# Sixteen weight pieces at sixteen offsets: moving the operands of a matmul kernel by bytes

## The chip, the cores and the metric

The kernel runs on one core of one Trainium2 chip. The metric is the device time of one execution in microseconds (us), as the median of the runs shown. Engines: PE is TensorE (PEld its weight loads), DVE VectorE, ACT ScalarE, POOL GpSimd, SP SyncE.

## What is computed

A retention layer (attention without softmax, with a decay by distance), followed by two feed-forward layers of 512 to 2048 to 512 over 2304 tokens:

```python
scores = scale * np.matmul(q, k.transpose(0, 1, 3, 2))   # 4 x 8 heads, 576 x 576, head_dim 64
ret = scores * Dmat                                      # gamma ** (row - column), causal
x = np.matmul(ret, v)                                    # laid out as (2304, 512)
h = x @ w_in;  x = np.maximum(0.01 * h, h) @ w_out       # first layer
h = x @ w_in2; x = (h - np.tanh(h)) @ w_out2             # second layer
```

The four weight matrices arrive as 64-bit floats and are narrowed on the chip.

## The kernel before

Every product of the two layers is made of three matmuls in float32r (fp32r): each operand is split into a high part and a low part, and high x high, low x high and high x low are summed in PSUM. x lies in SBUF for the whole kernel as `xh` and `xl`, [128, 4, 2304] each, and `acc` holds the sum over groups.

**Weights.** Each matrix is cut into 16 pieces f of 128 x 512 elements: `w_in` by its output columns, `w_out` by its rows. A piece is loaded (`load_piece`, on the SP queue), narrowed by five instructions (`narrow_ops`, lines 111 to 156, on DVE and partly ACT), and split by `split_piece` (line 171): ACT writes the high part to `wp[:, 0, :]` (line 174), POOL the low part to `wp[:, 1, :]` (line 175). `wp` is a tile of the pool `wring` with four buffers for the input pieces (tag w0) and four for the output pieces (tag w1). So four input and four output pieces, one "group", are in place at a time; a layer has four groups. Some narrowed pieces of the second layer are written to DRAM during the first and fetched back later.

**Layers.** A step (m, g, t0, n, f) is layer m, group g, a block of n tokens (512, or 256 for the last block) and one piece f of the group. `h_mm` (line 187, matmul in line 194) makes 12 matmuls, 4 slices of x by 3 products, with the weight slice as the stationary operand and `xh` or `xl` as the moving one. `act_a` and `chain` make from it `g`, high and low. `o_mm` (line 245, matmul in line 266) makes 12 matmuls with the output piece: in the first layer the weight slice is stationary and g moves, in the second g is stationary and the whole 512-wide row of the piece moves (6 matmuls where n is 256). `evac` adds into `acc`. In the loop of `layers`, step s issues `h_mm(s)` and then `o_mm(s - 2)`, so PE alternates between 12 input and 12 output matmuls, in an order that is written out by hand (`tc.manual_schedule`). Group 0 of the first layer has the 512-block and the 256-block alone in this loop; every other group has four 512-blocks and the 256-block.

**Retention and early units.** The 16 head pairs are worked off in `retention`. Beside the later ones, the first six 256-token blocks of group 0 of the first layer are done in 12 "units" of two pieces each: `unit_h` (24 matmuls of 256 columns, line 516; pieces 0 and 1 in even units, 2 and 3 in odd ones) and `unit_o` (24, line 541), with g tiles of a pool of their own.

**Places in SBUF.** Tiles lie one after another in the order of their pools, rounded to 32 bytes. In each partition the program has: the Pool DMA scratch at byte 0 (16,384 bytes), four constants and `qb` (32 bytes each), `xh` at 16,544, `xl` at 53,408, `acc` at 90,272, the eight `wp` buffers at 127,136 + 4096 s for s = 0 to 7 (s = 0 to 3 for input pieces, 4 to 7 for output pieces), the stage, and then the pools of either phase: the layers' `g` at 188,576 and two more 4096 apart, the early units' `g` at 213,088 and 217,184. The input pieces f mod 4 = 0, 1, 2, 3 get the buffers s = 0, 3, 2, 1, the output pieces 4, 7, 6, 5. All DMAs are issued with `nc.sync` or `nc.scalar`; none by POOL.

Of the kernel before, what the change touches and what calls it, by code (L numbers as in the profile page):

```python
# [11 lines left out]
F32R = mybir.dt.float32r  # L12
# [6 lines left out]
P = 128  # L19
CH = 128  # L20

TANH_T = 0.5
RHO_C = 0.0020447001866573740
RHO_V = 5.4327571340882842
# [7 lines left out]
def retention_moe_moe(  # L34
# [16 lines left out]
    nc = tc.nc  # L51
# [12 lines left out]
    wring = ctx.enter_context(tc.tile_pool(name="wring", bufs=GF))  # L64
# [105 lines left out]

    def split_piece(key):
        wf = half.pop(key)
        wp = wring.tile([P, 2, 512], F32R, tag=f"w{key[1]}", name="wp")
        nc.scalar.activation(out=wp[:, 0, :], in_=wf, func=AF.Copy)  # L174
        nc.gpsimd.tensor_tensor(  # L175
            out=wp[:, 1, :], in0=wf, in1=wp[:, 0, :].bitcast(F32), op=ALU.subtract
        )
        wt[key] = wp
# [132 lines left out]
    def piece_ops(keys, split=True, spare=()):  # L311


        ops, late = [], []
        for j, key in enumerate(keys):
            part = narrow_ops(key)
            if j + 2 < len(keys):
                part.append(lambda k=keys[j + 2]: load_piece(k))
            ops += part[:3] + late + part[3:]
            late = [lambda k=key: split_piece(k)] if split else []  # L320
            if key in spare:
                late = [lambda k=key: keep_piece(k)]
        return ops + late


    def retention():
        with ExitStack() as ac:
# [265 lines left out]
            nc.vector.memset(qb[:, 0:1], -RHO_V * math.sqrt(RHO_C))  # L593
            nc.vector.memset(qb[:, 1:2], -TANH_T * TANH_T)
            nc.scalar.activation(out=qb[:, 3:4], in_=qb[:, 2:3], func=AF.Tanh)
# [31 lines left out]
    def layers():  # L627
        with ExitStack() as mc:
# [35 lines left out]
            for s in range(n_early, end):  # L664
                h_mm(s)
                tight = s >= end - GF
                if tight:
                    act_a(s)
                if s > n_early:
                    chain(s - 1)  # L670
                if not tight:
                    act_a(s)
                if n_early <= s - LAG < end - GF:
                    o_mm(s - LAG)
                ops = plan.get(s, [])
                for op in ops[:4]:
                    op()
                if n_early <= s - LAG < end - GF:
                    evac(s - LAG)
                for op in ops[4:]:  # L680
                    op()
                for key in splits.get(s, ()):
                    split_piece(key)
# [79 lines left out]
```

## Time and profile before

| what | value |
|---|---|
| runs | 892.84 and 893.32 us, median 893.08 |
| profiled execution, first to last instruction (span) | 889.4 us |
| what lies around the span (median less span) | 3.7 us |
| busy in the span: PE, PEld | 863.9, 740.8 us |
| busy in the span: DVE, ACT, POOL | 532.8, 374.3, 422.5 us |
| mean granted TensorE clock | 0.995 |

The span is that of one execution under the profiler; the times above it are of runs without it. The end of a matmul's record is modelled, so that records overlap: the pace of matmuls is read from the distance of their starts. In the chain of waits, a piece "x12" is twelve instructions one behind another, and its time is their share of the chain.

### The profile page before, as it was taken

The numbers are of one execution on the slowest core, as the hardware profiler recorded it, in microseconds if no ns is written. First come the engines' busy times: TensorE is split into PE (matmuls) and PEld (weight loads), VectorE is DVE, ScalarE is ACT, GpSimd is POOL, SyncE is SP. The second block draws the span as 40 slices with busy tenths as digits, with TensorE's granted clock in tenths as the row PEclk, the third lists the DMA queues.
The fourth block names the chain that finished last, engine by engine and source line by source line (L and its number), as shares of the span: only waits on it lengthen the run. The fifth ranks groups of instructions, "written<-read, shape, count | busy, mean of one in ns | idle before, by whom it ended". The sixth has DMA issues, their size and how long they took to land.

```text
span 889.4 us, 13456 instructions
## 1 busy us (share of the span) xinstructions
PE 863.9 (97%) x5152; PEld 740.8 (83%) x5152; DVE 532.8 (60%) x880; ACT 374.3 (42%) x751; POOL 422.5 (48%) x340
## 2 busy tenths in 40 slices
PE   6669999999999999999999999999999999999998
PEld 5669999988888889888888888888888888888886
DVE  6964343698888788865652555444545655555454
ACT  2333222242122212233324665675466555565553
POOL 4644432264233622363224644585457744585443
PEclk9989999999999999999999999999999999999999
DMA  8743342233464335531121200020001000001111
GB/s 299 237 141 118 108 132 78 71 108 106 131 185 149 120 128 148 173 107 48 48 83 39 57 1 1 8 76 13 1 1 47 13 1 1 1 1 48 48 48 71
DMA packets 28576, 70.97 MB, mean 80 GB/s; under 512 B 3297, under 2 KB 3681, under 8 KB 28513
## 3 DMA queue, kind: packets, MB, share of 16 engines
q1 hardware_dynamic: 27936, 69.74, 24.5%
q8 instruction: 40, 0.66, 0.3%
q10 hardware_dynamic: 576, 0.38, 0.1%
q14 instruction: 24, 0.19, 0.1%
HBM read 59.10 MB, written 11.01 MB: 79 GB/s over the span
## 4 chain that ended last, share of the span: by engine, by line
PE 92%; DVE 3%; ACT 1%; DMA 1%; POOL 1%; issue 1%; SPq 0%; ACTq 0%; POOLq 0%
PE h L194 41%; PE a L266 40%; PE a L541 4%; PE x_b L516 3%; PE o L463 1%; PE sc L402 1%; PE o L475 1%; DVE cw L148 1%; DVE pt L417 1%; DMA kv<-in_vn 1%; POOL wp L175 1%; PE x_c L435 1%; DMA qk<-in_qT 1%; PE x_a L408 0%; DVE st L445 0%
## 5 line engine op out<-in xcount | busy, mean ns | idle before, releaser
L194 PE MATMUL h<-xh,wp 128*128 128x512 f32 (+1 forms) x1184 | 355.2, 366 | 0.0
L194 PEld LDWEIGHTS h<-xh,wp 128*128 128x128 f32 x1184 | 216.1, 189 | 37.0
L194 PE MATMUL h<-xl,wp 128*128 128x512 f32 (+1 forms) x592 | 216.9, 366 | 0.0
L266 PE MATMUL a<-wp,g 128*128 128x512 f32 x864 | 209.4, 390 | 0.2 <-POOL g L240 0.2
L266 PEld LDWEIGHTS a<-wp,g 128*128 128x128 f32 x864 | 161.1, 188 | 33.8 <-POOL g L240 1.0
L266 PE MATMUL a<-g,wp 128*128 128x512 f32 (+1 forms) x816 | 175.6, 364 | 0.0
L240 POOL TENSOR_TENSOR g<-v,g 128x512 fp32r<-128x512 f32 (+1 forms) x80 | 94.8, 1186 | 144.6 <-ACT g L239 144.5
L266 PEld LDWEIGHTS a<-g,wp 128*128 128x128 f32 x816 | 141.4, 189 | 24.6
L240 POOL TENSOR_TENSOR g<-a,g 128x512 fp32r<-128x512 f32 (+1 forms) x68 | 88.0, 1294 | 154.9 <-ACT g L208 141.5
L207 ACT ACTIVATE a<-h 128x512 f32<-128x512 f32 (+1 forms) x68 | 37.3, 548 | 227.0 <-PE h L194 226.1
L175 POOL TENSOR_TENSOR wp<-cw,wp 128x512 fp32r<-128x512 f32 x64 | 90.9, 1430 | 76.1 <-ACT wp L174 75.7
L194 PEld LDWEIGHTS h<-xl,wp 128*128 128x128 f32 x592 | 111.6, 189 | 18.5
L148 DVE SCALAR_TENSOR_TENSOR cw<-st,cw 128x512 uint32<-128x512 uint32 x128 | 115.2, 900 | 3.8
L233 DVE TENSOR_TENSOR h<-h,t 128x512 f32<-128x512 f32 (+1 forms) x80 | 51.5, 644 | 107.3 <-ACT t L217 107.3
L292 DVE TENSOR_TENSOR acc<-a,acc 128x512 f32<-128x512 f32 (+1 forms) x114 | 73.8, 662 | 66.8 <-PE a L266 66.7
L239 ACT ACTIVATE g<-v 128x512 fp32r<-128x512 f32 (+1 forms) x80 | 47.1, 589 | 145.4 <-DVE v L237 144.3
L218 POOL TENSOR_TENSOR v<-t,u 128x512 f32<-128x512 f32 (+1 forms) x80 | 94.8, 1185 | 14.2 <-ACT t L217 13.8
L234 DVE SCALAR_TENSOR_TENSOR v<-q,v 128x512 f32<-128x512 f32 (+1 forms) x80 | 55.5, 694 | 55.2 <-POOL v L218 54.1
L237 DVE COPY_PREDICATED v<-mk,h 128x512 f32<-128x512 uint32 (+1 forms) x80 | 54.9, 686 | 8.2
L219 ACT ACTIVATE q<-u,qb 128x512 f32<-128x512 f32 (+1 forms) x80 | 54.5, 681 | 0.0
L222 ACT ACTIVATE mk<-u,qb 128x512 f32<-128x512 f32 (+1 forms) x80 | 54.2, 677 | 0.0
L216 ACT ACTIVATE u<-h 128x512 f32<-128x512 f32 (+1 forms) x80 | 43.6, 545 | 19.4 <-PE h L194 18.9
(60 smaller groups left out, 774.5 us busy)
## 6 DMA issues: line engine op xcount, KB each, us to landing
st<-in_w1i SPq DMA_DIRECT2D x16, 512.0 KB, 3.6
st<-in_w1o SPq DMA_DIRECT2D x16, 512.0 KB, 3.5
st<-in_w2i SPq DMA_DIRECT2D x16, 512.0 KB, 4.0
st<-in_w2o SPq DMA_DIRECT2D x16, 512.0 KB, 4.0
kept<-cw SPq DMA_DIRECT2D x24, 256.0 KB, 4.3
cw<-kept SPq DMA_DIRECT2D x24, 256.0 KB, 2.7
kv<-in_vn SPq DMA_DIRECT2D x16, 320.0 KB, 5.1
qk<-in_qT SPq DMA_DIRECT2D x16, 288.0 KB, 4.0
```

The source lines that it names most:

```text
L148: nc.vector.scalar_tensor_tensor(out=t["w"], in0=t[src], scalar=scalar, in1=t["w"], op0=op, op1=ALU.bitwise_or)
L175: nc.gpsimd.tensor_tensor(out=wp[:, 1, :], in0=wf, in1=wp[:, 0, :].bitcast(F32), op=ALU.subtract)
L194: nc.tensor.matmul(out=ps[:, :n], lhsT=w[:, wi, cs], rhs=x[:, kk, t0:t0 + n], start=kk == 0 and i == 0, stop=kk == KK - 1 and i == 2,)
L218: nc.gpsimd.tensor_tensor(out=v[:, :n], in0=t_[:, :n], in1=u[:, :n], op=ALU.mult)
L219: nc.scalar.activation(out=q[:, :n], in_=u[:, :n], func=AF.Square, scale=math.sqrt(RHO_C), bias=qb[:, 0:1])
L222: nc.scalar.activation(out=mk[:, :n], in_=u[:, :n], func=AF.Relu, bias=qb[:, 1:2])
L233: nc.vector.tensor_tensor(out=h, in0=h, in1=t_, op=ALU.subtract)
L234: nc.vector.scalar_tensor_tensor(out=v, in0=q, scalar=RHO_A, in1=v, op0=ALU.add, op1=ALU.mult)
L237: nc.vector.copy_predicated(out=v, mask=mk.bitcast(U32), data=h)
L240: nc.gpsimd.tensor_tensor(out=gt[:, 1, :n], in0=v, in1=gt[:, 0, :n].bitcast(F32), op=ALU.subtract)
L266: nc.tensor.matmul(out=o, lhsT=l, rhs=r, start=f == 0 and i == 0 and d % pack == 0, stop=f == GF - 1 and i == 2 and (d + 1) % pack == 0, s ...
L292: nc.vector.tensor_tensor(out=dst, in0=a, in1=dst, op=ALU.add)
```

## The change

Each piece gets a buffer of 1136 elements a partition (4544 bytes) in place of 1024, and begins in it at an offset of its own, by f: 0, 16, 32, ... 112 bytes for f = 0 to 7, then 128, 256, 384, 4, 8, 192, 320, 448. ACT, POOL and PE address the same [128, 2, 512] view as before, at that offset. To make room, the scratch for DMAs of POOL, at the bottom of SBUF, shrinks from 16,384 to 1024 bytes.

```diff
+PLACES = (0, 4, 8, 12, 16, 20, 24, 28, 32, 64, 96, 1, 2, 48, 80, 112)
...
     def split_piece(key):
         wf = half.pop(key)
-        wp = wring.tile([P, 2, 512], F32R, tag=f"w{key[1]}", name="wp")
+        at = PLACES[key[2] % len(PLACES)]
+        room = wring.tile([P, 1024 + max(PLACES)], F32R, tag=f"w{key[1]}", name="wp")
+        wp = room[:, at:at + 1024].rearrange("p (i d) -> p i d", i=2)
         nc.scalar.activation(out=wp[:, 0, :], in_=wf, func=AF.Copy)
...
-    nc = bacc.Bacc("TRN2", target_bir_lowering=False, num_devices=1)
+    nc = bacc.Bacc("TRN2", target_bir_lowering=False, num_devices=1, dynamic_dma_scratch_size=1024)
```

## Rows read from the trace of the kernel before

**Rows 1.** The page: its span, the busy time, and the chain by line.

```profile
span 889.4 us, 13456 instructions
...
PE 863.9 (97%) x5152; PEld 740.8 (83%) x5152; DVE 532.8 (60%) x880; ACT 374.3 (42%) x751; POOL 422.5 (48%) x340
...
PE h L194 41%; PE a L266 40%; PE a L541 4%; PE x_b L516 3%; PE o L463 1%; PE sc L402 1%; PE o L475 1%; DVE cw L148 1%; DVE pt L417 1%; DMA kv<-in_vn 1%; POOL wp L175 1%; PE x_c L435 1%; DMA qk<-in_qT 1%; PE x_a L408 0%; DVE st L445 0%
```

**Rows 2.** Chain in order of time (start, us, what): both layers.

```profile
203.56 2.72 PE a L266 x12
206.28 2.72 PE h L194 x12
...
614.45 2.72 PE a L266 x12
```

**Rows 3.** Chain in order of time: an early unit.

```profile
94.80 2.88 PE x_b L516 x24
97.67 2.74 PE a L541 x24
```

**Rows 4.** Timeline of PE, 98 to 99.95 us (start, us, engine, line, count).

```profile
97.75 2.43 PE L541 MATMUL a<-g,wp 128*128 128x256 f32 x20
```

**Rows 5.** The instructions of tile wp: min/median/max in ns.

```profile
L541 PEld LDWEIGHTS a<-g,wp x288: 186/188/338, 50.3 to 161.7; 128*128 128x128 f32 x144
L541 PE MATMUL a<-g,wp x288: 276/276/582, 50.4 to 161.8; 128*128 128x256 f32 x144
L516 PEld LDWEIGHTS x_b<-xh,wp x192: 186/192/193, 36.7 to 153.8; 128*128 128x128 f32 x192
L516 PE MATMUL x_b<-xh,wp x192: 277/283/388, 36.8 to 154.0; 128*128 128x256 f32 x192
...
L174 ACT ACTIVATE wp<-cw x64: 615/630/645, 21.9 to 798.6; 128x512 fp32r<-128x512 f32 x64
L175 POOL TENSOR_TENSOR wp<-cw,wp x64: 1264/1300/1783, 23.0 to 799.3; 128x512 fp32r<-128x512 f32 x64
```

**Rows 6.** Timeline, line view and windows, line 541 near 59 us (0.50 is PEclk).

```profile
58.78 1.70 PE L541 MATMUL a<-g,wp 128*128 128x256 f32 x7
...
L541 PE MATMUL a<-g,wp x8: 415/415/420, 58.6 to 60.1; 128*128 128x256 f32 x8
...
59.00:60.10 1.10, 1.10 (x7) 0.50 0.00 0
```

**Rows 7.** Timeline, 97.3 to 97.6 us: a matmul and the next one's weight load.

```profile
97.27 0.28 PE L516 MATMUL x_b<-xl,wp 128*128 128x256 f32 x1
97.27 0.19 PEld L516 LDWEIGHTS x_b<-xh,wp 128*128 128x128 f32 x1
```

**Rows 8.** The page's groups of matmuls of the layers.

```profile
L194 PE MATMUL h<-xh,wp 128*128 128x512 f32 (+1 forms) x1184 | 355.2, 366 | 0.0
...
L194 PE MATMUL h<-xl,wp 128*128 128x512 f32 (+1 forms) x592 | 216.9, 366 | 0.0
L266 PE MATMUL a<-wp,g 128*128 128x512 f32 x864 | 209.4, 390 | 0.2 <-POOL g L240 0.2
...
L266 PE MATMUL a<-g,wp 128*128 128x512 f32 (+1 forms) x816 | 175.6, 364 | 0.0
```

**Rows 9.** Chain in order of time: 512-wide steps behind 256-wide ones.

```profile
173.44 1.43 PE a L266 x12
174.88 2.75 PE h L194 x12
```

**Rows 10.** Chain in order of time: the end of the last early unit.

```profile
160.88 1.18 PE a L541 x10
```

**Rows 11.** What PE waited for: us in total, times, longest.

```profile
PE a L541 <- ACT wp L174: 4.9, 1, 4.9
```

**Rows 12.** Timeline of PE, 174.7 to 177.4 us; five matmuls from first to last.

```profile
174.71 0.40 PE L194 MATMUL h<-xh,wp 128*128 128x512 f32 x1
...
175.87 0.61 PE L194 MATMUL h<-xh,wp 128*128 128x512 f32 x2
```

## The prediction

> **What bounds the kernel now.** I read the page first: of a span of 889.4 us TensorE (PE) is busy 863.9, and the chain of work that ended last lies on PE for the two big lines 194 and 266 (41% and 40%), with lines 541 and 516 next [rows 1]. The other engines are busy 60% or less, so only PE's own pace can move the end by per cents. Second, the chain in order of time. In both layers a step of 12 matmuls, 512 columns wide, takes 2.72 us, the same for line 194 and line 266, for first layer and second [rows 2]: 226.7 ns a matmul. The granted clock is 1.0 there (the 2.4 GHz level), so 512 columns at one a cycle are 213.3 ns; 13.3 ns a matmul are something else, and that is what an address could change.
>
> Third, the same operation at 256 columns, where the kernel happens to hold two relations of addresses. Line 516 (input matmuls of the early units) takes 2.88 us for 24, or 120.0 ns each; line 541 (output matmuls of the same units) takes 2.74 us for 24 [rows 3], and within such a run 20 matmuls span 2.43 us [rows 4], the last of them being 0.276 long by itself [rows 5], so (2.43 - 0.276) / 19 = 113.4 ns each. Bare streaming would be 256 / 2.4 = 106.7. The excess is 13.3 on line 516 and 6.7 on line 541, with the same width, type, number of products and weight buffers. The tile view has it too: the median matmul record is 283 ns on 516 and 276 on 541, the weight load 192 against 188 [rows 5].
>
> What differs is where the operands lie. In the program's own allocation xh and xl begin at byte 160 modulo 512 of a partition, the eight weight buffers also at 160 (they are 4096 apart), the layers' g also at 160, but the early units' g at 96. Call "distance" the start of the weight operand minus the start of the x or g operand, modulo 512. All slices step by multiples of 512, and the pace doesn't depend on which slice it is; so distance 0 costs 13.3 ns and distance 64 costs 6.7. At the lower clock level (granted 0.50, 1.2 GHz) line 541 took (1.70 - 0.415) / 6 = 214 ns a matmul [rows 6], which is bare streaming (256 / 1.2 = 213.3): two streams at a fixed relation that do not meet. I read the excess as the weight load of the next matmul, which starts as the running one does (both at 97.27 us) [rows 7], meeting the moving stream in the memory, once at distance 64 and twice at distance 0. That reading is inferred from two distances only.
>
> **The change, part by part.** No instruction, wait, DMA or queue order is added or moved. Three things change.
>
> The smaller scratch moves every tile down by 15,360 bytes, 30 x 512. No DMA in the kernel is issued by POOL. The larger buffers (8 x 448 bytes more) push what lies behind them by 11,776 bytes in all, 23 x 512. So x and both g stay at 160, 160 and 96: cost nothing.
>
> The weight pieces move. Buffers are now 4544 bytes apart, which is 64 short of a multiple of 512, so buffer s adds -64 s to the offset in PLACES. The buffers are taken in the order 0, 3, 2, 1 by the input pieces f mod 4 = 0, 1, 2, 3, and 4, 7, 6, 5 by the output pieces. That gives, for f = 0 to 15, input distances 0, 336, 416, 496, 64, 400, 480, 48, 128, 64, 256, 452, 8, 0, 192, 384, and output distances (sign aside) 256, 80, 160, 240, 320, 144, 224, 304, 384, 320, 0, 196, 264, 256, 448, 128. I take 64 bytes or more either way as far enough to save 6.7 ns, and less as saving nothing.
>
> Input: f = 0 to 3 have 7 steps each in the layers (2 + 5, as six blocks went to the early units), the others 10; 148 steps x 12 = 1776 matmuls, which are the 1184 + 592 of the page [rows 8]. Far enough are f = 1, 2 (14 steps) and 4, 5, 8, 9, 10, 14, 15 (70): 84 x 12 = 1008 matmuls. Output: 864 + 816 = 1680 [rows 8], all but f = 10, which has 5 x 12 + 4 x 12 + 6 = 114: 1566 matmuls. Together 2574 x 6.67 ns = 17.2 us. The early units add f = 1 and 2 of line 516, 2 x 6 x 12 = 144 matmuls, 1.0 us; line 541 would go from distance 64 to 320, 144, 224, 304, no change. All of it lies on the chain [rows 1, 3].
>
> Against that stands a start cost. When the relation changes between two runs of matmuls, the pace takes some matmuls to settle: line 541's 24 take 2.74 us and not 24 x 113.4 = 2.72, so 20 ns [rows 3, 4]; a 512-wide step behind a 256-wide one takes 2.75 and not 2.72 [rows 2, 9], so 30. Now input and output steps alternate at constant distance; then nearly each of 296 steps begins at a new one: 296 x 0.020 = 5.9 us, bounds 0 and 296 x 0.030 = 8.9.
>
> The saving is bounded too. The last run of line 541, which began after PE had stood idle, kept 1.18 / 10 = 118 ns at the same distance 64 [rows 10], a saving of only 2 ns; by that the sum would be 2718 x 2 = 5.4 us. I take 6.67, because every other run at the full clock shows 113, and because the layers, like these, have PE never idle. No row shows a 512-wide matmul at another distance: the bounds for it are 0 and the whole 13.3.
>
> The fine offsets: f = 11 and 12 begin 4 and 8 bytes off. No row shows such an operand. A weight load of 188 ns [rows 5] has 226.7 to hide in; as moving operand of the second layer (2 x 54 matmuls) the nearest dear row is the lower clock's pace, 100 ns more per 256 columns, so 0 to 21 us; I take 0, as the rows for aligned slices are nearer. The writers of the pieces, ACT 630 ns and POOL 1300 [rows 5], are hidden under the matmuls, except in the first group, where PE waited up to 4.9 us at once for them [rows 11]; if they became slower by a tenth, that is 0.5 us. I take 0.
>
> Sum: -17.2 - 1.0 + 5.9 = -12.3. The profiled span is 889.4 and the runs' median 893.08, so 3.7 lie around the span and stay. Span 877.1, time 880.8, say 881. With the bounds of the start cost and of the saving the case's own range is 875 to 891.
>
> **The rivals.** *Nothing changes at 512 columns.* The 13.3 ns would then be a fixed cost of a matmul with a new weight, and 541's 113 a matter of 256-wide matmuls, where load and stream are equally long. For it: 2.72 in every full step whatever the buffer. Against it: all those steps have distance 0, and 512 and 256 show the same 13.3. Time 893, less 1.0 at most. The Trainium skill sides with this rival: "TensorE: Matmul & The Clock Gate", in the section "Step-by-step: what each phase is for", gives TensorE two independent read ports, so that loading the next weights takes nothing from the running matmul; by that the sum is 0. The 283 against 276 ns of the trace speak against it, as far as two addresses can.
>
> *More is saved.* Near pieces gain also, and nothing is lost at the starts: (1776 + 1680 + 288) x 6.67 = 25 us, 868; with the start costs gone alone, 875; if the far ones lost all 13.3, 857. For it: the clean 214 at the lower clock. Against it: distance 64 still costs 6.7. The same page (section "Back-to-back issue gap") has N / 2.4 + 2.5 ns, 215.8 at 512; by that floor 3456 x 10.9 = 37.7 us would go, an estimate that no run here shows.
>
> *Slower.* Some distances are worse than 0. The mechanism is seen where a 512-wide step follows a 256-wide one: five matmuls from 174.71 to 175.87 us, 232 ns each [rows 12], 5.3 more than settled. If the streams meet oftener at mid distances, such matmuls keep 232. All 3456 so: +18.3, time 911; a third gaining and two thirds losing, with the start cost: -7.7 + 12.2 + 5.9, time 904. It decides from where under 44% of the matmuls gain (5.3 / 12), or 58% with the start cost. Against it: the one other distance seen is better.
>
> **How the numbers follow.** Forecast case 0.38, nothing changes 0.20, more is saved 0.27, slower 0.15. The range 867 to 900 leaves out the far end of the third case and the upper half of the last. Faster by over 2% (under 875.2; about what a measurement here can tell from no change) is nearly all of the third case and a little of the first: 0.29; slower by over 2% (over 911) the worst of the last case or dear fine offsets: 0.07; within 2% the rest, 0.64.
>
> **What would show it.** In the changed chain, steps of line 194 and 266 should no longer all take 2.72 us: far pieces 2.64 plus up to 0.03, near ones 2.72, sorted by f and the same in both layers. Line 516's 24 should fall for the f = 1 and 2 halves; line 541 should stay at 2.74. Steps of 2.72 everywhere make the distance no cause; steps over 2.75 would show worse distances, and over 3 us for f = 11 or 12 on line 266 of the second layer dear fine offsets. A wait of PE for wp in the layers would mean that ACT or POOL slowed down.

## The result: slower by 1.5%, and the profile after

The changed kernel takes 906.28 us (906.24 and 906.32) where the kernel before took 893.08; the ratio is 1.0149 with a 95% interval of 1.0120 to 1.0179. The forecast was 881, in a range of 867 to 900: wrong in sign, and outside the range.

The page of the changed kernel, to be read against [rows 1]:

```profile
span 904.5 us, 13456 instructions
...
PE 877.8 (97%) x5152; PEld 741.9 (82%) x5152; DVE 529.0 (58%) x880; ACT 376.2 (42%) x751; POOL 418.6 (46%) x340
...
PE h L197 41%; PE a L269 40%; PE a L544 4%; PE x_b L519 3%; PE sc L405 1%; PE o L478 1%; PE o L466 1%; DVE cw L149 1%; DVE pt L420 1%; DVE cw L138 1%; POOL wp L178 1%; PE x_c L438 1%; DVE st L448 0%; DMA qt_sb<-in_qtab 0%; ACT bd L394 0%
```

The span grew by 15.1 us and PE's busy time by 13.9, with the same instructions and the same shares of the chain (lines 194, 266, 516, 541 are now 197, 269, 519, 544). Nothing new is waited for: PE itself became slower. The chain in order of time, inside the first layer, answers to [rows 2]:

```profile
273.61 2.80 PE a L269 x12
276.41 2.79 PE h L197 x12
279.20 2.80 PE a L269 x12
282.00 2.80 PE h L197 x12
```

Steps of 2.72 us have become 2.80: 233 ns a matmul in place of 226.7, though the pieces here (f = 4 to 7) lie at input distances of 64, 112, 32 and 48 either way and output distances of 192, 144, 224 and 208. By windows (PE busy first), the layers are the stretch from 164.2 us on, and from 161.9 on in the kernel before:

```profile
164.20:900.10 735.90, 735.73 (x3457) 609.27 (x3456) 442.54 (x667) 328.12 (x626) 350.51 (x284) 1.00 0.20 62
```

```profile
161.90:885.00 723.10, 722.92 (x3457) 609.29 (x3456) 448.13 (x667) 326.11 (x626) 354.51 (x284) 1.00 0.20 63
```

The layers grew by 12.8 us of the 15.1, at the same granted clock of 1.00. The start of the layers lies 2.3 us later, but over the runs of this study it lies anywhere between 161.6 and 164.2 us, whatever the distances. From the distance of matmul starts in the layers, the 2880 matmuls of 512 columns took 654.3 us before and 667.8 after (+13.5), the 576 of 256 columns 68.9 and 68.1 (-0.8). By piece, most 512-wide steps take 2.75 to 2.80 us. For seven pieces the matmuls come back to the old 226.7 ns before a step ends, some at its start and some only after ten slower ones: at distance 0 (input pieces 0 and 13, output piece 10), at 256 (input piece 10, output pieces 0 and 13) and at 16 the other way, which is 496 (input piece 3). One step stands against any rule by distance alone: input piece 5 (distance 400), whose steps take 2.79 or 2.80 us, ran once in the second layer at 226.7 ns from its first matmul to its last. The chain has it first, and then the next block's step with the same piece:

```profile
599.31 2.72 PE h L197 x12
...
621.59 2.80 PE h L197 x12
```

The early units, in the chain, answer to [rows 3]:

```profile
96.66 2.83 PE x_b L519 x24
99.49 2.84 PE a L544 x24
```

Here the 256-wide input matmuls became a little faster (2.88 to 2.83), and the output ones, which the forecast left at 2.74, slower.

### The profile page after: what moved, and what is told of

It is laid out like the page before. It is cut to its first block, busy times and chain, and to the rows that moved or that the text cites. A ratio compares the mean times of both kernels' runs of the same rounds, so it can differ in the third digit from the quotient of the medians.

```text
span 904.5 us, 13456 instructions
## 1 busy us (share of the span) xinstructions
PE 877.8 (97%) x5152; PEld 741.9 (82%) x5152; DVE 529.0 (58%) x880; ACT 376.2 (42%) x751; POOL 418.6 (46%) x340
## 4 chain that ended last, share of the span: by engine, by line
PE 92%; DVE 4%; ACT 1%; POOL 1%; issue 1%; DMA 0%; ACTq 0%; POOLq 0%
PE h L197 41%; PE a L269 40%; PE a L544 4%; PE x_b L519 3%; PE sc L405 1%; PE o L478 1%; PE o L466 1%; DVE cw L149 1%; DVE pt L420 1%; DVE cw L138 1%; POOL wp L178 1%; PE x_c L438 1%; DVE st L448 0%; DMA qt_sb<-in_qtab 0%; ACT bd L394 0%
## 5 line engine op out<-in xcount | busy, mean ns | idle before, releaser
L197 PE MATMUL h<-xh,wp 128*128 128x512 f32 (+1 forms) x1184 | 359.1, 369 | 0.0
L269 PE MATMUL a<-wp,g 128*128 128x512 f32 x864 | 213.4, 394 | 0.2 <-POOL g L243 0.2
L269 PE MATMUL a<-g,wp 128*128 128x512 f32 (+1 forms) x816 | 178.3, 367 | 0.0
L178 POOL TENSOR_TENSOR wp<-cw,wp 128x512 fp32r<-128x512 f32 x64 | 87.7, 1378 | 87.2 <-ACT wp L177 87.0
L237 DVE SCALAR_TENSOR_TENSOR v<-q,v 128x512 f32<-128x512 f32 (+1 forms) x80 | 51.3, 641 | 51.4 <-POOL v L221 50.4
```

The source lines that it names most:

```text
L178: nc.gpsimd.tensor_tensor(out=wp[:, 1, :], in0=wf, in1=wp[:, 0, :].bitcast(F32), op=ALU.subtract)
L197: nc.tensor.matmul(out=ps[:, :n], lhsT=w[:, wi, cs], rhs=x[:, kk, t0:t0 + n], start=kk == 0 and i == 0, stop=kk == KK - 1 and i == 2,)
L237: nc.vector.scalar_tensor_tensor(out=v, in0=q, scalar=RHO_A, in1=v, op0=ALU.add, op1=ALU.mult)
L269: nc.tensor.matmul(out=o, lhsT=l, rhs=r, start=f == 0 and i == 0 and d % pack == 0, stop=f == GF - 1 and i == 2 and (d + 1) % pack == 0, s ...
```

## The experiments

### All pieces at one distance: 0, or 64

Against the changed kernel (the second has `at = 16`, elements of 4 bytes):

```diff
-        at = PLACES[key[2] % len(PLACES)]
-        room = wring.tile([P, 1024 + max(PLACES)], F32R, tag=f"w{key[1]}", name="wp")
+        at = 0
+        room = wring.tile([P, 1152], F32R, tag=f"w{key[1]}", name="wp")
```

> The changed kernel with every piece at the start of its buffer, buffers 4608 bytes apart (9 x 512), the scratch still small: every distance between a weight operand and its x or g operand is 0 modulo 512, as before. Distance theory (the pace depends on the distance, and 0 is a good one for 512 columns): 12-matmul steps of 2.72 us and 893 us in all, within 2 us. Rival (larger buffers, smaller scratch or the shifted addresses cost the time): 906 us, as the changed kernel.

> As the run before, but every piece 64 bytes into its buffer: one and the same distance (64) everywhere. Distance theory: 512-wide matmuls at 231 to 234 ns in all steps, 256-wide ones at 113 to 118; 2880 x 6 ns = +17 us, less 576 x 5 ns = 3 us in the layers and 1 us in the early units: 904 to 909 us. Start-cost rival (only the change of distance from step to step costs): no step differs from its neighbour, so 893 or less. The piece's own place (rival: only where the piece lies counts) expects the same as the distance theory; the fourth run tells these apart.

Measured: at 0, 892.45 us, ratio 0.9995 (0.9986 to 1.0005); at 64, 906.16 us, ratio 1.0139 (1.0124 to 1.0154). The chain at 0, and then at 64:

```profile
201.20 2.72 PE h L197 x12
203.92 2.72 PE a L269 x12
```

```profile
201.34 2.80 PE h L197 x12
204.14 2.80 PE a L269 x12
```

Larger buffers, the small scratch and the shifted addresses cost nothing; a constant distance of 64 costs all that the sixteen different ones did. So the loss is not the price of going from one distance to another. And 64 is where the forecast expected a gain: at 256 columns it is one (the early units' input matmuls, at 64):

```profile
95.39 2.74 PE x_b L519 x24
98.13 2.85 PE a L544 x24
```

2.88 fell to 2.74 on line 519, and line 544, now at distance 128, rose from 2.74 to 2.85. At 512 columns the same distance of 64 is bad. Nor does 64 always give 113 ns at 256 columns: in this run the 256-wide matmuls of the first layer took 113.5 ns, those of the second layer (line 197) 117.8.

### One distance for each group: a table

From here on the diffs are against the kernel with all pieces at 0, where nothing else is said.

```diff
-        at = 0
+        at = (0, 4, 8, 16, 24, 32, 48, 60)[key[0] * 4 + key[2] // GF]
```

The second kernel has (0, 1, 2, 64, 40, 44, 52, 56).

> One offset for all eight pieces of a group, another for each of the eight groups (four of the first layer, then four of the second): 0, 16, 32, 64, then 96, 128, 192, 240 bytes. Distance theory: the steps of a group settle to one pace, 226.7 ns at 0, and by the pieces of the changed kernel about 233 at 32 to 128, 229 to 232 at 192, 227 to 229 at 240 (which is -16); 902 to 906 us in all. Start-cost rival: all groups settle to 226.7 and the time stays near 893.

> One offset for all pieces of a group: 0, 4, 8, 256 bytes in the first layer, 160, 176, 208, 224 in the second. Distance theory with period 256, and 0 to 16 as good as 0: 226.7 ns at 512 columns at 0, 4, 8 and 256, near 233 at the other four; about 900 us. Rival 1 (an operand that begins off a 16-byte boundary costs by itself): more than 227 at 4 and 8. Rival 2 (period 512): 231 to 234 at 256. If the good zone is as wide to the other side, 224 (which is -32) shows it by 227 on line 194.

Measured: 904.23 and 904.52 us. Mean ns from start to start of the 512-wide matmuls of a group, line 197 / line 269, by the offset of its pieces in bytes (in the second layer, from 96 in the first run and from 160 in the second, the piece is the moving operand in line 269, so the sign turns there):

| run | | | | | | | | |
|---|---|---|---|---|---|---|---|---|
| first, offset | 0 | 16 | 32 | 64 | 96 | 128 | 192 | 240 |
| ns | 228 / 227 | 227 / 228 | 233 / 233 | 233 / 233 | 234 / 234 | 233 / 233 | 232 / 233 | 229 / 234 |
| second, offset | 0 | 4 | 8 | 256 | 160 | 176 | 208 | 224 |
| ns | 228 / 228 | 232 / 232 | 231 / 231 | 227 / 228 | 234 / 234 | 230 / 232 | 232 / 233 | 233 / 234 |

The chain of the second run where the group at 8 bytes (line 269 first) gives way to the one at 256:

```profile
400.08 2.77 PE a L269 x12
402.85 2.72 PE h L197 x12
405.57 2.72 PE a L269 x12
```

Whole groups settle to a pace of their own, so the start-cost rival falls. 256 is as good as 0. 16 is good and 32 is not; 4 and 8 are not good either, which I had expected to be: whether the odd start or the distance of less than 16 does that, these runs do not separate. At 240 line 197 is nearly good and line 269 of the second layer, where the sign is the other, is not; I have no rule for that. Nowhere is a 512-wide group faster than the same group in the kernel with all pieces at 0 (226.7 to 228.4 ns): the kernel before stood at the best place of all that were tried.

### Moving x alone, and moving everything

```diff
+    keep.tile([P, 16], F32, name="pad")
     xh = keep.tile([P, KK, NT], F32R, name="xh")
...
+    keep.tile([P, 112], F32, name="pad2")
```

Against the kernel before; the second kernel has the first pad alone, so that x, pieces and g all move by 64 bytes. (`acc` moves in both; no matmul reads it.)

> The kernel before with xh and xl alone moved by 64 bytes (a pad ahead of xh, 448 bytes behind acc); the weight pieces and g keep their places modulo 512. Distance theory: line 194 goes to distance -64 (192), its 512-wide steps to 2.76 to 2.80 us (229 to 233 ns) and its 256-wide matmuls to 114 to 118 ns, line 266 stays at 2.72; 896 to 900 us. Rival (the weight piece's own place decides): no weight piece has moved, so line 194 stays at 2.72 and the time at 893.

> The kernel before with a 64-byte pad ahead of xh, and nothing behind it: x, weight pieces and g all move by 64 bytes together, every distance stays 0. Distance theory: steps of 2.72 us for lines 194 and 266 and 893 us. Rival (the place of an operand itself, 160 modulo 512, is the good one): all steps near 2.80 us, 905 us or more.

Measured: 902.74 us with x moved, 893.29 with all moved (the kernel before gave 893.62 and 891.28 beside them). The chain with x moved, lines 196 and 268, and with all moved:

```profile
219.61 2.76 PE h L196 x12
222.37 2.77 PE a L268 x12
```

```profile
202.91 2.72 PE h L195 x12
205.63 2.72 PE a L267 x12
```

No weight piece moved in the first of these kernels, and line 196 still went to 2.76; everything moved in the second, and nothing happened. So it is the relation of the two operands' places that counts, and not the place of either by itself. The miss is line 268: its operands are at distance 0 as before, yet it went from 2.72 to 2.77. The differences of its starts in one such step, in ns, show why:

```
234 230 234 236 224 231 236 228 233 230 227 227
```

It needs ten matmuls to come back to 227 after a step at another distance: a start cost of some 50 ns a step, where the forecast had 20 to 30 [rows 3, 4, 9]. Good steps of the changed kernel come into the same row of gaps at other places: one of output piece 13 has 234 236 224 231 235 229 232 231 and then 227. So the pace of a step depends on the state in which the step before left off, and not on its own distance alone. In kernels whose steps are all far, the start cost doesn't show; a good step between bad ones is often spoilt (2.72 to 2.79 us for input piece 13 in the changed kernel).

### Half a weight load

```diff
+                cols = P if kk == 0 and i == 0 else P // 2
                 nc.tensor.matmul(
-                    out=ps[:, :n], lhsT=w[:, wi, cs], rhs=x[:, kk, t0:t0 + n],
+                    out=ps[:cols, :n], lhsT=w[:, wi, kk * P:kk * P + cols],
+                    rhs=x[:, kk, t0:t0 + n],
```

> Distance 0 (all pieces at the start of buffers 4608 bytes apart). Of the 12 matmuls of a step of line 194 the first keeps its 128 weight columns, the other 11 load and use 64 only; half of the output columns of the input products are left out, so the layers' results are not the reference's. The moving operand stays 512 or 256 wide. Meeting theory (the excess comes from the weight load reading while the moving operand streams): half a load, so the excess of 13.3 ns falls to about half, 220 ns a matmul at 512 columns, and line 194 loses 1276 x 6.7 = 8.5 us. Rival (a fixed cost of changing the weights): 226.7 as in the run with all pieces at 0.

> As the run before (11 of 12 matmuls of line 194 with 64 weight columns, half of the input products left out), with every piece at distance 64. Meeting theory: the excess of 20 ns at 512 columns falls to about half, 223 ns a matmul on line 194, while line 266 with its full loads stays at 231 to 233. Rival (fixed cost, and distance acting on the moving operand alone): 233 on line 194.

Measured: 896.93 us at 0 and 904.80 at 64. The tile view of wp at 0 (min/median/max in ns) shows the short loads, 134 ns where a full one has 188:

```profile
L198 PEld LDWEIGHTS h<-xh,wp x1184: 133/134/192, 164.1 to 884.7; 128*64 128x64 f32 x148, 128*128 128x128 f32 x50
```

Its chain:

```profile
203.10 2.75 PE h L198 x12
205.85 2.74 PE a L272 x12
```

The meeting theory falls in the form it had: with half the columns to load, 512-wide matmuls took 229.5 ns at distance 0 and not 220, slower than with a full load, and 232 to 233 at 64. The 256-wide ones at 0 did fall, from 120 to 113.5, which is half of the excess, as that theory has it. So at 512 columns the excess is not so much for each piece of the load. These steps stand between steps with full loads, and their gaps at 0 (226 236 229 224 227 234 230 236 229 224 227 231 in one step) do not become even in twelve matmuls; what a longer row of half loads would take is not shown.

### The moving operand standing still

```diff
-                    out=ps[:, :n], lhsT=w[:, wi, cs], rhs=x[:, kk, t0:t0 + n],
+                    out=ps[:, :n], lhsT=w[:, wi, cs], rhs=x[:, kk, t0:t0 + 1].to_broadcast([P, n]),
```

> All pieces at 0; in line 197 the moving operand is one column of x read n times (a step of zero) instead of n columns, so the moving stream stands still in memory. The input products, and all that follows, are not the reference's. Relation theory (two streams walking through memory at some distance): line 197 no longer depends on the distance and loses part of its 13.3 ns: 213 to 227 ns, the same as in the run with pieces at 64. Rival (the 13.3 ns belong to the load or the change of weights alone): 226.7 as with x moving.

> As the run before (one column of x read n times, products not the reference's), with every piece at distance 64. Relation theory: line 197 at 512 columns has the same pace as in the run before, within 1 ns, while line 269 stays at 231 to 233. Rival (the weight load's own place costs): line 197 stays at 233.

Measured: 877.37 us at 0, 880.61 at 64. The chains:

```profile
205.31 2.59 PE h L197 x12
207.91 2.76 PE a L269 x12
```

```profile
206.85 2.59 PE h L197 x12
209.44 2.80 PE a L269 x12
```

In both, line 197 takes 215.8 ns at 512 columns and 111.5 at 256, while line 269, with moving operands that walk, still depends on the distance (and at 0 takes 2.76 and not 2.72, as it did with x moved). This splits the 13.3 ns of the kernel before: of the 226.7, 213.3 are streaming, 2.5 stay with a moving operand that stands still, and 10.9 come only when it walks through memory (17.4 at a distance of 64). At 256 columns 4.8 stay, and 8 to 9 come with the walk at distance 0. Of the 10.9, these runs show only that the walk brings them; that the weight load has a part in them is not shown. The Trainium skill ("TensorE: Matmul & The Clock Gate", section "Back-to-back issue gap") gives N / 2.4 + 2.5 for the gap of a matmul by itself, which is 215.8 at 512 columns and 109.2 at 256. The run agrees to the tenth at 512 columns and is 2.3 ns above it at 256; the 512-wide matmuls with moving operands that walk are all far above it, 226.7 and more.

### The low part 128 bytes further

```diff
-        wp = room[:, at:at + 1024].rearrange("p (i d) -> p i d", i=2)
+        wp = room[:, :1088].rearrange("p (i d) -> p i d", i=2)[:, :, :512]
```

> All pieces at 0, but the low part of each piece 128 bytes further behind the high part. In line 197 the products run (high, xh), (high, xl), (low, xh). If the running matmul and the load of the next one are the pair that counts, the distance is 128 while xl streams (the low part is being loaded), and the second of every three gaps grows; if a matmul and its own weights are the pair, the third grows. One third of the 512-wide matmuls at 233 in place of 227: 897 to 899 us by either, more if a changed distance disturbs the two others also (each change had cost a step some 50 ns in the run with x moved): up to 906.

Measured: 903.44 us. In line 197, from start to start, the gaps after (high, xh), (high, xl), (low, xh) repeat as

```
227 233 234
```

The timeline of PE shows the first two, 309.18 to 309.40 and on to 309.64:

```profile
309.18 0.39 PE L197 MATMUL h<-xh,wp 128*128 128x512 f32 x1
309.40 0.40 PE L197 MATMUL h<-xl,wp 128*128 128x512 f32 x1
309.64 0.62 PE L197 MATMUL h<-xh,wp 128*128 128x512 f32 x2
```

Each theory had one gap grow, the second or the third; both did. In line 269 of the second layer, where the low part is the moving operand of the third product, it is the third gap alone (227, 226, 235). Both patterns fit if a matmul is slow when either its own weights or those being loaded beside it are at a distance; that is a reading after the fact, and which of the two is at work, or whether one disturbance lasts for two gaps, stays open.

### Only narrow matmuls at 64

Against the kernel with all pieces at 0:

```diff
-        at = 0
+        at = 16 if key[:2] == (0, 0) and key[2] < GF else 0
...
+            gt = gt[:, :, 48:48 + n] if n == 256 else gt
             nc.scalar.activation(out=gt[:, 0, :n], in_=h, func=AF.Prelu, alpha=0.01)
```

> From the kernel with all pieces at 0: only 256-wide matmuls are put at distance 64, where the pieces of the changed kernel and the run with all pieces at 64 had them at 113 to 114 ns in place of 120: the four input pieces of the first group of the first layer (at 64, for line 519 of the early units) and g of the first layer's 256-wide steps (192 bytes into its tile). Distance theory: line 519's runs go from 2.88 to 2.74 us, 11 runs on the chain give 1.5 us; line 269's 256-wide steps from 1.44 to 1.37, 16 x 0.07 = 1.1 us, part of it given back at the 512-wide steps beside them; 890 to 892 us where the kernel before has 893, a version a little faster than both. Rival (the early units are bound elsewhere, or neighbours give all of it back): 893 to 894.

Measured: 891.82 us, ratio to the kernel before 0.9983 (0.9972 to 0.9993). The chain of the early units:

```profile
94.93 2.74 PE x_b L520 x24
97.67 2.83 PE a L545 x24
```

Line 520 gave the 0.14 us a run that was expected. Line 545 gave most of it back: 2.83 where it had 2.74 [rows 3], with its own operands at the same distance 64 as before; it now follows matmuls of another relation, and stays in another rhythm for all of its 24. The 256-wide steps of the first layer's output products (line 270 here) went from 119.7 to 116.2 ns. The whole is 0.17% faster than the kernel before.

## Why the prediction was wrong

The reading of the profile held in its first half. PE's own pace decides; the excess over streaming changes with the distance between the weight operand and the other one (shown by x moved, all moved, and the table); scratch and buffer sizes cost nothing (the run with all pieces at 0). The writers of the pieces cost nothing either: in the changed kernel's trace their medians are those of [rows 5], and PE has no wait for them in the layers.

```profile
L177 ACT ACTIVATE wp<-cw x64: 615/630/642, 23.0 to 811.3; 128x512 fp32r<-128x512 f32 x64
L178 POOL TENSOR_TENSOR wp<-cw,wp x64: 1087/1299/1814, 23.7 to 812.0; 128x512 fp32r<-128x512 f32 x64
```

The step that failed is "I take 64 bytes or more either way as far enough to save 6.7 ns", applied to 512-wide matmuls. At 512 the distance of 64 takes 6.5 ns more, not 6.7 less. The term of -17.2 us, which has both widths in it, came out as +12.7 with the start costs of 5.9 in it (+13.5 at 512 columns, -0.8 at 256). At 256 columns it was right for the early units' input (113 ns at 64) and not in general: 117.8 ns at 64 in the second layer, and with x moved, which is 64 the other way, 118. So the sign, which "either way" sets aside, matters too, and the 118 ns of [rows 10], taken as the exception, is a pace that comes back. The prediction said itself that no row showed a 512-wide matmul at another distance, and then bounded that case by 0 and 13.3 saved: only gains. The bound on the other side stood in [rows 12], 232 ns for five matmuls in a 512-wide step, and was used for the slower rival alone. That rival, priced at 232 ns and 904 us, is what happened (233 ns at most distances, 906 us), though its mixture was another: 7 of the 32 pieces came back to the good pace at 512 columns, and the 256-wide matmuls gained 0.8 us. Its reason, streams that meet oftener at mid distances, is not shown. The case's own range of 875 to 891 does not come out of its bounds either: a saving of 5.4 against a start cost of 8.9 gives an upper end of 896.6.

The early units' 1.0 us of gain came out as a loss of some 0.6 us: from the third run on, a run of line 519 became at most 0.05 us shorter and one of line 544 0.05 to 0.11 longer. The output distances of 320, 144, 224 and 304, which the forecast put down as no change, run at 118 ns on average where 64 had run at 113.4.

The start cost exists and was put too small by half for a good step behind a bad one (some 50 ns against 20 to 30), but as nearly all steps became bad it carried little of the sum. The fine offsets cost next to nothing: output piece 11, 4 bytes off, takes 2.86 us a step as the moving operand where its neighbours take 2.80, 5 steps in all, 0.3 us; the bound was 21.

"Nothing changes at 512 columns" falls: 226.7 or 233 ns with nothing changed but where the pieces lie, 215.8 with a moving operand that stands still. The Trainium skill ("TensorE: Matmul & The Clock Gate", section "Step-by-step: what each phase is for") has two independent read ports, so that a weight load takes nothing from the running matmul. These runs speak against it in so far as the places of the two operands relative to each other change the pace; that it is the load which takes time from the stream is argued and not shown. My picture of how (so many meetings of load and stream) fell at 512 columns with the half load. Why 0, 16 and 256 are good for 512 columns, why 64 is good for 256 columns, and why a rhythm depends on the one before it, is open.

## What to carry to other kernels

Where PE is the bound, look at the distance of matmul starts against columns / clock: here 20 ns of 233, over 8%, were not streaming, and 6.5 of them a matter of where operands lie. Where the matmuls are 512 columns wide in fp32r, as most are here, keep stationary and moving operands at the same place modulo 256 bytes (4096-byte tiles and slices of 512 did that here without anyone asking); for 256 columns the best place seen was another, 64. Re-read the pace after any change of tile sizes or of what lies ahead in SBUF, even one that seems to be of no concern to PE. And bound a price that no row shows from both signs: two distances at one width said nothing of another width.

## What the runs showed that was not expected

A row of identical matmuls has several stable rhythms: line 541 in the kernel before, and line 545 in the last experiment, with the same operands at the same distance, ran at 113.4 and at about 118 ns. Moving one operand by 64 bytes is worth 1.0% of this kernel (902.74 us), moving all of them nothing. A half-sized weight load, in steps between steps with full loads, made a 512-wide matmul slower by 3 ns. And a moving operand that repeats one column streams at 215.8 ns, 5% under the best walking pace.
